# Retention, Mish layer and GELU layer in one kernel: two weight chunks in retention, second parts on GpSimd, scores of two units together

## The chip, the cores and the metric

The kernel runs on one core of a Trainium2 chip. The metric is the device time of one execution in microseconds (us), the median of three runs. The program is written out in full: every engine has its own list of instructions in a fixed order, and waits only where an instruction needs something that another engine or a transfer has not finished.

## The reference

Three steps, in float32. Retention: for each of 4 batches and 8 heads, scores of 576 positions, times a causal decay, times the values. Then two feed-forward layers over the 2304 tokens, the first with Mish, the second with a sigmoid form of GELU.

```python
scores = scale * np.matmul(q, k.transpose(0, 1, 3, 2))     # (4, 8, 576, 576), head size 64
Dmat = np.where(rel >= 0, gamma[:, None, None] ** rel, 0)  # gamma of each head
attn = np.matmul(scores * Dmat, v)
x = attn.transpose(0, 2, 1, 3).reshape(2304, 512)
h = x @ w_in;  x = (h * np.tanh(softplus(h))) @ w_out      # 512 -> 2048 -> 512
h = x @ w_in2; x = (h / (1 + np.exp(-1.702 * h))) @ w_out2 # 512 -> 2048 -> 512
```

## The kernel before, in words

**Retention** works in 20 units: 4 batches of 5 chunks of the sequence, four of 128 positions and a last one of 64 (units 4, 9, 14 and 19). One transfer brings a unit's q, k, v and k again (`load`, line 715). A unit goes through these steps: GpSimd multiplies v by its decay in place (`decay_v`, line 767); TensorE forms the scores (`scores`, line 778) and VectorE masks them into `pm` (line 782); TensorE adds the unit's keys and values to the running sum of its batch (`update`, line 801, not for the 64 wide chunk); ScalarE copies that sum to the state (`take`); TensorE forms the outputs from the state of the unit before (line 829, not for the first chunk of a batch) and from `pm` and v (line 840); VectorE scales them into X (`finish`, line 854). Five buffers hold units, so the load of unit u+4 waits for the last outputs of unit u-1. `pm` has four buffers, two per unit, and the scores use four banks, two per unit.

The scores of unit u+1 are issued ahead of the sum and the outputs of unit u, from unit 2 on.

**The Mish layer's inputs** are held as two parts, a rounded one and the rest: ScalarE writes the first part of X, VectorE subtracts it from X for the second (`split_x`, line 335). This is done for one quarter of the first token block in each of units 4 to 7 (512 columns), and for the second block in units 8 to 11 (256 columns).

**The Mish layer's weights** come in 16 chunks (`w1`, 1 MB each; tile `raw`). Each half of a chunk goes through six steps, tied by named places in the program ("vector", "act early", "pool", "act late"): VectorE clamps it (line 183), ScalarE does two conversions, VectorE does two integer steps (lines 128 and 195), GpSimd joins them (line 199), ScalarE writes the first part, VectorE subtracts for the second (line 236). In each pass of the unit loop, a place runs what is due there, so a half moves about one unit per step. The first three chunks are converted during retention: `fetch` at units 0, 4 and 8, the conversion's first step 5 units later. The other chunks are due at `LATE`, in steps of the Mish layer, where step 2m needs chunk m.

In one pass of the unit loop, GpSimd's list gets `decay_v(u + 1)`, then the joins that are due. VectorE's gets the masks of the unit whose scores are issued there, `finish(u)`, then the conversion steps, then the input's second part. ScalarE's gets `take(u)`, the conversions, the write of a first part of weights, then the input's first part.

**The Mish layer** starts at the end of retention: `up(0)` is issued after unit 17, `up(1)` after unit 18, then `layers()` alternates `up(i)` (line 348) and `down(i - 3)` (line 369). The GELU layer (lines 592 and 637) follows. Neither is touched by the change, other than by the due times of the weight chunks.

Of the kernel before, what the change touches and what calls it, by code (L numbers as in the profile page):

```python
# [22 lines left out]
NK = DM // P  # L23
NM = DFF // P
# [8 lines left out]
SIDE, WIDTH = 1, 256  # L33
# [26 lines left out]

KEPT = 10
X_UNITS = (4, 5, 6, 7, 8, 9, 10, 11)
EARLY = 3
EARLY_EVERY, EARLY_AFTER = 4, 5
LATE = [1 + 1.95 * i for i in range(NM - EARLY)]
UNITS_AHEAD = 4
GROW = (16, 32, 64)
TABLES = NCH * H + NPAIR * (NCH + len(GROW) + GROW[0])
# [29 lines left out]
def retention_mish_gelu_kernel(ctx: ExitStack, tc: tile.TileContext, qkv, w1, w2, tables, out):  # L98
    nc = tc.nc
# [57 lines left out]
    def place(m):  # L157
        return keep if m < KEPT else late[0]

    def fetch(m):  # L160

        raw = place(m + 1).tile([P, 2 * DM], I64, tag=f"w{m + 1}", name="raw")
        if m < EARLY:
            nc.sync.dma_start(out=raw, in_=w1[m])
# [128 lines left out]
    n_u = len(UNITS)  # L293
# [3 lines left out]
    def plan_conversion(m, s, every):  # L297

        for i in range(2):
            last[0] = max(math.ceil(s + i * every / 2), last[0] + (i == 0))  # L300
            plan("fetch" if m == NM - 1 else "vector", last[0] - (m == NM - 1), convert(m, i))

    for m in range(EARLY):
        u = EARLY_EVERY * m
        plan("fetch", u - n_u, fetch(m))
        plan_conversion(m, u + EARLY_AFTER - n_u, 2)
    for m, s in zip(range(EARLY, NM), LATE):
        if m < NM - 1:
# [15 lines left out]
    def split_x(t, k):  # L324

        o, n = BLOCKS[t]
        if t == SIDE:
            if k % 2 == 0:
                side.append(keep.tile([P, 2, 2, WIDTH], F32R, tag=f"side{k // 2}", name="side"))
            x = side[-1][:, k % 2]  # L330
        else:
            x = keep.tile([P, 2, NB], F32R, tag=f"x{k}", name=f"x{k}")
        xs[t, k] = x
        act(x[:, 0, :n], X[:, k, o : o + n])
        return lambda: nc.vector.tensor_tensor(  # L335
            out=x[:, 1, :n], in0=X[:, k, o : o + n], in1=x[:, 0, :n].bitcast(F32), op=ALU.subtract
        )

# [360 lines left out]
    def attention():  # L699
        with tc.tile_pool(name="att", bufs=1) as ap:  # L700
# [59 lines left out]
                load(u)  # L760
            pm, sums, now = {}, [None], [None]

            def decay_v(u):
                b, c = UNITS[u]
                n = CH[c][1]
                vv = loaded[u][2][:n].rearrange("p (h d) -> p h d", d=D)
                nc.gpsimd.tensor_tensor(
                    out=vv, in0=vv, in1=vt[:n, c, :].unsqueeze(2).to_broadcast([n, H, D]), op=ALU.mult
                )

            def scores(u):
                n = CH[UNITS[u][1]][1]
                qt, kt = loaded[u][:2]
                sc = [quarters(bank("sc", (0, 1, 2, 3))) for _ in range(2)]
                for p in range(NPAIR):
                    for j in range(2):
                        sl = slice(64 * j, 64 * j + 64)
                        nc.tensor.matmul(sc[j][:n, p, :n], lhsT=kt[sl, p, :], rhs=qt[sl, p, :], start=True, stop=True)  # L778
                pm[u] = []
                for j in range(2):  # L780
                    t = ap.tile([P, NPAIR, P], F32, tag="pm", name="pm", bufs=4)
                    nc.vector.tensor_tensor(  # L782
                        out=t[:n, :, :n],
                        in0=sc[j][:n, :, :n],
                        in1=cm[:n, :n].unsqueeze(1).to_broadcast([n, NPAIR, n]),
                        op=ALU.mult,
                    )
                    pm[u].append(t)
# [67 lines left out]
                )  # L856

            scores(0)
            decay_v(0)
            for u in range(n_u):  # L860
                step = u - n_u
                load(u + UNITS_AHEAD)
                if u + 1 < n_u:
                    decay_v(u + 1)
                position("pool", step)
                position("fetch", step)
                if 1 < u < n_u - 1:
                    scores(u + 1)
                update(u)
                now[0], before = take(u), now[0]  # L870
                o = outputs(u, before)
                if u == 1:
                    scores(u + 1)
                if u < NCH - 1:
                    n = CH[u + 1][1]
                    for p in range(NPAIR):
                        act(gt[:, u + 1, p, :n], gt[:, 0, p, :n], scale=steps[:, p, u + 1 : u + 2])
                position("act early", step)

                if u == n_u - 2:  # L880
                    elementwise(0, jobs=False)
                finish(u, o)
                if u == n_u - 1:
                    elementwise(1, jobs=False)
                if u == 0:
                    scores(1)
                position("vector", step)
                position("act late", step)
                if u in X_UNITS:
                    k = X_UNITS.index(u)  # L890
                    split_x((0, SIDE)[k // NK], k % NK)()
                if u == n_u - 3:
                    up(0)
                if u == n_u - 2:
                    up(1)
# [97 lines left out]
```

## Time and profile before

| | |
|---|---|
| median of 3 runs | 821.23 us (820.43 to 821.35) |
| the profiled execution | 821.12 us |
| its span | 819.4 us, 1.7 us below its time |
| TensorE busy in the span | 811.4 us, 99% |
| VectorE, ScalarE, GpSimd busy | 550.1, 406.2, 113.2 us |
| granted TensorE clock | the top digit, 9, in all of the page's 40 slices |
| chain that ended last | TensorE 93%, DMA 3%, VectorE 3% |

The span is the time in which the profile saw instructions. The chain that ended last is followed back from the last instruction to what released each step; it says which engine a moment of the span belongs to. Busy time of TensorE alone says little here, since matmuls are pipelined and a matmul that waits in the array counts as busy.

### The profile page before, as it was taken

How to read it: one execution, taken by the hardware profiler on the slowest of the kernel's cores; microseconds unless marked ns; L12 is line 12 of the kernel's file. 1: busy time of each engine (PE TensorE's matmuls, PEld its weight loads, DVE VectorE, ACT ScalarE, POOL GpSimd, SP SyncE). 2: the span in 40 equal slices, each digit the busy share in tenths (PEclk: the TensorE clock that was granted, in tenths of full speed). 3: DMA queues.
4: the chain of work that ended last, by engine and by line, in shares of the span. 5: the costliest groups of instructions: out<-in, count | busy, mean ns of one | idle time of the engine just before them, and what ended most of it. 6: DMA issues, size and time to landing. Idle time of an engine off the chain costs nothing.

```text
span 819.4 us, 13441 instructions
## 1 busy us (share of the span) xinstructions
PE 811.4 (99%) x5094; PEld 740.3 (90%) x5094; DVE 550.1 (67%) x1030; ACT 406.2 (50%) x748; POOL 113.2 (14%) x123
## 2 busy tenths in 40 slices
PE   8999999999999999999999999999999999999998
PEld 6888888888888888788888899999999999999998
DVE  4895566665876766787655455789645798555776
ACT  4553666664455556455443333465233665233553
POOL 3552222222122212133210000000000000000000
PEclk9999999999999999999999999999999999999999
DMA  9999700003477739678621277777877887877775
GB/s 344 400 334 368 281 1 2 1 1 103 142 239 221 246 116 257 193 202 264 188 78 64 102 261 251 258 259 252 325 250 237 274 272 256 306 252 247 261 266 168
DMA packets 96048, 175.01 MB, mean 214 GB/s; under 512 B 5232, under 2 KB 67312, under 8 KB 90096
## 3 DMA queue, kind: packets, MB, share of 16 engines
q1 hardware_dynamic: 95696, 173.89, 63.4%
q8 instruction: 40, 0.66, 0.3%
q10 hardware_dynamic: 288, 0.27, 0.1%
q14 instruction: 24, 0.20, 0.1%
HBM read 140.05 MB, written 34.08 MB: 213 GB/s over the span
## 4 chain that ended last, share of the span: by engine, by line
PE 93%; DMA 3%; DVE 3%; POOL 0%; issue 0%; ACT 0%; SPq 0%; POOLq 0%; DVEq 0%
PE h L348 24%; PE acc L369 23%; PE p L592 21%; PE p L637 21%; DMA unit<-qkv_dram 2%; PE o L840 1%; PE sc L778 1%; DVE pm L782 1%; PE o L829 1%; DMA stream<-cy 1%; PE ds L801 1%; DVE x L335 0%; DVE X L854 0%; DVE w L236 0%; DVE side L335 0%
## 5 line engine op out<-in xcount | busy, mean ns | idle before, releaser
L369 PE MATMUL acc<-g,w 128*128 128x512 f32 (+1 forms) x960 | 209.5, 368 | 0.0
L369 PEld LDWEIGHTS acc<-g,w 128*128 128x128 f32 x960 | 168.3, 188 | 30.4
L348 PE MATMUL h<-x,w 128*128 128x512 f32 x768 | 184.9, 390 | 0.3 <-DVE x L335 0.2
L592 PE MATMUL p<-xop,ring 128*128 128x384 f32 x1008 | 175.2, 334 | 0.0
L637 PE MATMUL p<-g,ring 128*128 128x384 f32 x1008 | 175.2, 334 | 0.0
L592 PEld LDWEIGHTS p<-xop,ring 128*128 128x128 f32 x1008 | 174.8, 188 | 0.1
L637 PEld LDWEIGHTS p<-g,ring 128*128 128x128 f32 x1008 | 174.8, 188 | 0.0
L348 PEld LDWEIGHTS h<-x,w 128*128 128x128 f32 x768 | 143.8, 188 | 31.0 <-DVE x L335 1.1
L398 DVE TENSOR_TENSOR g<-c,g 128x512 fp32r<-128x512 f32 x80 | 53.2, 664 | 110.2 <-ACT g L119 110.2
L119 ACT ACTIVATE g<-cs 128x384 fp32r<-128x384 f32 x168 | 87.9, 524 | 63.2 <-PE p L637 61.2
L430 DVE TENSOR_TENSOR g<-cs,g 128x384 fp32r<-128x384 f32 x168 | 92.5, 557 | 26.1 <-ACT g L119 25.0
L119 ACT ACTIVATE g<-c 128x512 fp32r<-128x512 f32 x80 | 47.1, 589 | 123.3 <-PE acc L369 122.9
L119 ACT ACTIVATE cs<-cs 128x384 f32<-128x384 f32 x72 | 37.9, 526 | 111.8 <-DVE cs L430 111.8
L199 POOL TENSOR_TENSOR cy<-cr 128x256 int32<-128x256 int32 x64 | 51.9, 831 | 177.5 <-DVE cr L195 96.5
L119 ACT ACTIVATE c<-h 128x512 f32<-128x512 f32 x80 | 44.1, 551 | 47.4 <-PE h L348 44.9
L430 DVE TENSOR_TENSOR cs<-cs 128x384 f32<-128x384 f32 x96 | 53.1, 553 | 0.8
L199 POOL TENSOR_TENSOR raw<-raw 128x512 int32<-128x512 int32 x30 | 34.4, 1147 | 98.5 <-DVE raw L195 93.1
L119 ACT ACTIVATE cr<-cr 128x512 int32<-128x512 uint32 x68 | 41.5, 664 | 1.3 <-DVE cr L183 1.3
L430 DVE TENSOR_TENSOR u<-p,s 128x384 f32<-128x384 f32 x30 | 16.7, 556 | 34.9 <-PE p L592 34.9
L119 ACT ACTIVATE raw<-raw 128x512 int32<-128x512 uint32 (+1 forms) x60 | 37.8, 674 | 4.6 <-DVE raw L183 4.4
L284 DVE TENSOR_TENSOR cy<-cy,cr 128x896 fp32r<-128x896 f32 x32 | 36.8, 1155 | 2.7 <-ACT cr L119 1.7
L277 DVE TENSOR_TENSOR cy<-cy 128x128 f32<-128x128 f32 x96 | 26.1, 299 | 13.3 <-POOL cy L199 12.2
(63 smaller groups left out, 644.6 us busy)
## 6 DMA issues: line engine op xcount, KB each, us to landing
ring<-stream SPq DMA_DIRECT2D x112, 512.0 KB, 4.5
ring<-stream SPq DMA_DIRECT2D x28, 1024.0 KB, 4.8
cr<-w_dram SPq DMA_DIRECT2D x34, 512.0 KB, 4.4
unit<-qkv_dram SPq DMA_DIRECT2D x15, 1024.0 KB, 8.2
stream<-cr SPq DMA_DIRECT2D x32, 448.0 KB, 2.8
stream<-cy SPq DMA_DIRECT2D x32, 448.0 KB, 3.3
raw<-w_dram SPq DMA_DIRECT2D x24, 512.0 KB, 10.4
raw<-w_dram SPq DMA_DIRECT2D x3, 1024.0 KB, 10.5
```

The source lines that it names most:

```text
L119: nc.scalar.activation(out=o, in_=i, func=f, scale=scale, bias=bias)
L199: nc.gpsimd.tensor_tensor(out=o, in0=upper, in1=bits, op=ALU.add)
L277: nc.vector.tensor_tensor(out=v[:, o], in0=v[:, a], in1=v[:, b], op=op)
L284: nc.vector.tensor_tensor(out=y, in0=v, in1=hi.bitcast(F32), op=ALU.subtract)
L348: nc.tensor.matmul(h[:, :n], lhsT=W[m][:, a, k * P : (k + 1) * P], rhs=xs[t, k][:, b, :n], start=((k, a, b) == order[0]), stop=((k, a, b) ...
L369: nc.tensor.matmul(acc[t, e][:, :n], lhsT=W[m][:, a, DM + e * P : DM + (e + 1) * P], rhs=g[:, b, :n],  start=(begins(i) and a == 0 and b = ...
L398: lambda: nc.vector.tensor_tensor(out=g[:, 1, :n], in0=c[:, :n], in1=g[:, 0, :n].bitcast(F32), op=ALU.subtract),
L430: eng.tensor_tensor(out=o, in0=a, in1=b, op=op)
L592: nc.tensor.matmul(banks[p], lhsT=w[:, a, k * P : (k + 1) * P], rhs=x[:, b, k], start=(p not in SAME and k == 0 and a == 0 and b == 0), st ...
L637: nc.tensor.matmul(banks[e, p], lhsT=w[:, a, e * P : (e + 1) * P], rhs=g[:, b], start=(p != 2 and r == 0 and a == 0 and b == 0), stop=(r = ...
L778: nc.tensor.matmul(sc[j][:n, p, :n], lhsT=kt[sl, p, :], rhs=qt[sl, p, :], start=True, stop=True)
L782: nc.vector.tensor_tensor(out=t[:n, :, :n], in0=sc[j][:n, :, :n], in1=cm[:n, :n].unsqueeze(1).to_broadcast([n, NPAIR, n]), op=ALU.mult,)
```

## The change

The table of early chunks is cut to two (the second fetched at unit 6, not 4), and the later chunks' due times start three steps earlier, so that chunk 2 is due at step -2, which is unit 18. The second parts of the inputs go to GpSimd. The decay of unit 0's v goes to VectorE. From unit 2 on, the scores are issued for two units together, behind the outputs of every even unit.

```diff
-EARLY = 3
-EARLY_EVERY, EARLY_AFTER = 4, 5
-LATE = [1 + 1.95 * i for i in range(NM - EARLY)]
+EARLY = 2
+EARLY_EVERY, EARLY_AFTER = 6, 5
+LATE = [-2 + 1.95 * i for i in range(NM - EARLY)]
...
-        return lambda: nc.vector.tensor_tensor(
+        return lambda eng=nc.vector: eng.tensor_tensor(
             out=x[:, 1, :n], in0=X[:, k, o : o + n], in1=x[:, 0, :n].bitcast(F32), op=ALU.subtract
         )
...
-            def decay_v(u):
+            def decay_v(u, eng=nc.gpsimd):
...
-                nc.gpsimd.tensor_tensor(
+                eng.tensor_tensor(
...
-            decay_v(0)
+            decay_v(0, nc.vector)
...
-                if 1 < u < n_u - 1:
-                    scores(u + 1)
                 update(u)
                 now[0], before = take(u), now[0]
                 o = outputs(u, before)
                 if u == 1:
                     scores(u + 1)
+                elif u and u % 2 == 0:
+                    for n in (u + 1, u + 2):
+                        if n < n_u:
+                            scores(n)
...
-                    split_x((0, SIDE)[k // NK], k % NK)()
+                    split_x((0, SIDE)[k // NK], k % NK)(nc.gpsimd)
```

GpSimd's list around units 8 to 10. The `unit` rows are the decays of units 8, 9 and 10, the `raw` rows the joins of the two halves of weight chunk 0. Before:

```order
L767 TENSOR_TENSOR unit_306<-unit_306,tab_75 128x512
L199 TENSOR_TENSOR raw_118<-raw_118 128x512
L767 TENSOR_TENSOR unit_346<-unit_346,tab_75 64x512
L199 TENSOR_TENSOR raw_118<-raw_118 128x512
L767 TENSOR_TENSOR unit_389<-unit_389,tab_75 128x512
```

and with the change (here the decays of units 8, 9 and 10 are `unit_306`, `unit_358` and `unit_387`; `x3` and `side` are second parts of the input):

```order
L767 TENSOR_TENSOR unit_306<-unit_306,tab_75 128x512
L199 TENSOR_TENSOR raw_118<-raw_118 128x512
L335 TENSOR_TENSOR x3_494<-X_60,x3_494 128x512
L767 TENSOR_TENSOR unit_358<-unit_358,tab_75 64x512
L199 TENSOR_TENSOR raw_118<-raw_118 128x512
L335 TENSOR_TENSOR side_559<-X_60,side_559 128x256
L767 TENSOR_TENSOR unit_387<-unit_387,tab_75 128x512
```

Each decay now stands behind a subtraction, which reads what ScalarE wrote.

VectorE's list from the masks of unit 7 to the first integer steps on chunk 0. Before (`sc_392` and `sc_393` are the scores of unit 7, `o_416` the outputs of unit 6):

```order
L335 TENSOR_TENSOR x1_386<-X_60,x1_386 128x512
L782 TENSOR_TENSOR pm_402<-sc_392,cm_76 128x512
L782 TENSOR_TENSOR pm_404<-sc_393,cm_76 128x512
L854 TENSOR_TENSOR X_60<-o_416,gt_79 128x4x128
L128 SCALAR_TENSOR_TENSOR raw_118<-raw_118 128x512
L195 TENSOR_SCALAR raw_118<-raw_118 128x512
L183 TENSOR_SCALAR raw_118<-raw_118 128x512
L335 TENSOR_TENSOR x2_439<-X_60,x2_439 128x512
```

and with the change (`sc_419`, `sc_420` are unit 7's scores, `sc_433`, `sc_434` unit 8's, `o_402` and `o_470` the outputs of units 6 and 7):

```order
L183 TENSOR_SCALAR raw_118<-raw_118 128x512
L782 TENSOR_TENSOR pm_429<-sc_419,cm_76 128x512
L782 TENSOR_TENSOR pm_431<-sc_420,cm_76 128x512
L782 TENSOR_TENSOR pm_443<-sc_433,cm_76 128x512
L782 TENSOR_TENSOR pm_445<-sc_434,cm_76 128x512
L854 TENSOR_TENSOR X_60<-o_402,gt_79 128x4x128
L128 SCALAR_TENSOR_TENSOR raw_118<-raw_118 128x512
L195 TENSOR_SCALAR raw_118<-raw_118 128x512
L183 TENSOR_SCALAR raw_118<-raw_118 128x512
L854 TENSOR_TENSOR X_60<-o_470,gt_79 128x4x128
```

The subtractions are gone, and the integer steps of chunk 0 stand behind the masks of two units.

TensorE's list from the scores of unit 6 on, over the sums and outputs of units 5 and 6. Before:

```order
L778 MATMUL sc<-unit 128x128 x8
L801 MATMUL ds<-unit 64x64 x8
L840 MATMUL o<-pm,unit 64x128 x8
L778 MATMUL sc<-unit 128x128 x8
L801 MATMUL ds<-unit 64x64 x8
L829 MATMUL o<-unit,state_72 64x128 x8
L840 MATMUL o<-pm,unit 64x128 x8
```

and with the change (the first row is the scores of units 5 and 6):

```order
L778 MATMUL sc<-unit 128x128 x16
L801 MATMUL ds<-unit 64x64 x8
L840 MATMUL o<-pm,unit 64x128 x8
L801 MATMUL ds<-unit 64x64 x8
L829 MATMUL o<-unit,state_72 64x128 x8
L840 MATMUL o<-pm,unit 64x128 x8
L778 MATMUL sc<-unit 128x128 x16
```

The scores of two units stand together, and those of unit 7 now come behind the outputs of unit 6.

## Rows read from the trace of the kernel before

**Rows 1.** Busy time by stretch: engine busy us (instructions), granted clock, DMA share, GB/s

```profile
22.00:37.00 15.00, 14.87 (x290) 13.49 (x290) 13.34 (x23) 8.42 (x17) 6.42 (x6) 1.00 1.02 393
37.00:58.00 21.00, 20.39 (x372) 17.80 (x370) 20.82 (x37) 10.68 (x22) 13.30 (x10) 1.00 0.97 368
...
420.00:620.00 200.00, 200.00 (x1093) 192.01 (x1092) 122.52 (x216) 83.02 (x156) 0.00 (x0) 1.00 0.64 218
```

**Rows 2.** The chain of waits, TensorE and DMA pieces: start us, length us, what

```profile
9.93 11.97 DMA unit<-qkv_dram
...
24.51 1.16 PE sc L778 x16
...
30.62 1.09 PE sc L778 x16
31.71 0.61 PE ds L801 x16
32.33 0.88 PE o L829 x16
33.20 0.87 PE o L840 x16
34.08 0.61 PE sc L778 x16
...
66.17 2.97 PE h L348 x12
...
72.12 1.63 PE h L348 x12
73.74 0.62 PE o L829 x16
...
74.97 4.38 PE h L348 x24
79.35 2.75 PE acc L369 x12
```

**Rows 3.** The same chain, VectorE pieces between 43 and 54 us

```profile
43.82 1.20 DVE pm L782 x2
45.02 0.60 DVE X L854
45.62 0.61 DVE raw L128
...
46.25 0.43 DVE raw L195
46.68 0.34 DVE raw L183
...
53.81 0.74 DVE pm L782 x2
```

**Rows 4.** GpSimd's instructions on tiles unit and raw: ns min/median/max

```profile
L767 POOL TENSOR_TENSOR unit<-unit,tab x20: 1035/1043/1897, 7.1 to 64.8; 128x512 f32<-128x512 f32 x16, 64x512 f32<-64x512 f32 x4
...
L199 POOL TENSOR_TENSOR raw<-raw x6: 1041/1150/1414, 32.5 to 62.8; 128x512 int32<-128x512 int32 x6
```

**Rows 5.** Timeline of ScalarE, 30 to 40 us: start us, length us, instruction

```profile
30.88 0.61 ACT L119 ACTIVATE x<-X 128x512 fp32r<-128x512 f32 x1
...
38.59 0.70 ACT L119 ACTIVATE w<-raw 128x512 fp32r<-128x512 f32 x1 [2.18 <-POOL raw L199]
39.18 0.73 ACT L119 ACTIVATE side<-X 128x256 fp32r<-128x256 f32 x2
```

**Rows 6.** Timeline of VectorE, unit 0's masks and two subtractions of one form

```profile
7.42 1.29 DVE L782 TENSOR_TENSOR pm<-sc,cm 128x512 f32<-128x512 f32 x2 [0.61 <-PE sc L778]
...
24.88 1.25 DVE L335 TENSOR_TENSOR x<-X,x 128x512 fp32r<-128x512 f32 x1
...
28.30 0.68 DVE L335 TENSOR_TENSOR x<-X,x 128x512 fp32r<-128x512 f32 x1
```

**Rows 7.** The first matmuls of the program, line 745: ns min/median/max

```profile
L745 PE MATMUL unused<-state x6: 593/1061/1222, 1.5 to 5.6; 128*128 128x512 f32 x6
```

## The prediction

> **What bounds the kernel now.** I read busy time by stretch first, then the chain of waits, then the timelines of the engines that hand work to each other. From the end of retention on there is nothing to win: TensorE is busy in every microsecond of 420 to 620 [rows 1], and the chain that ended last is TensorE's alone. So only retention, the first 75 us, can change, and with it the first steps of the Mish layer, where weights are still being converted. In 22 to 37 us TensorE is busy 14.87 of 15 us; in 37 to 58 VectorE is busy 20.82 of 21 and TensorE slips [rows 1].
>
> How much TensorE slips, I get from the chain [rows 2]. One unit costs it 1.09 (scores) + 0.61 (sum) + 0.88 + 0.87 (outputs) = 3.45 us; the first unit of a batch lacks the 0.88, and a 64 wide unit has 0.61 + 0.62 + 0.62 and no sum. Between the scores of unit 6 at 24.51 and `up(0)` at 66.17 stand 11 wide scores, 2 narrow ones, 11 sums and the outputs of units 5 to 17: 13.2 + 6.7 + 19.1 = 39.0 us. The stretch took 41.66, so **2.7 us** are lost there, nearly all while VectorE is full. From 66.17 to 74.97 nothing is lost: `up(0)`, `up(1)`, the rest of units 18 and 19 add up to 8.8. Before 24.51 data set the time: the chain shows 11.97 us of one load from 9.93 on [rows 2], and the DMA engines are still at a share of 1.02 in the next stretch [rows 1]. So I take 24.5 as the moment at which unit 6 can be had.
>
> **The change, part by part.**
>
> *First batch, unit 0's decay: 0.* On VectorE the decay stands behind two masks: these start at 7.42 [rows 6] and take 1.2 [rows 3], the product 0.6 more (0.68 for a like form [rows 6], of which 0.08 lies beside the next one). So unit 0's sum starts at 9.2. From there to the scores of unit 6 TensorE has 0.61 + 0.87 for unit 0, 3 x 3.45, 0.61 + 1.24 for unit 4 and 1.09 for the scores of unit 5, 14.8 us, which end at 24.0, and unit 6 comes at 24.5. If that cover of 0.5 us fails, the cost is at most the same 0.5. The second score of a pair waits for its own load: for unit 6 it is this same 24.5, later ones have slack, since a unit takes TensorE 3.45 us, and 1.05 MB at the 393 GB/s of this stretch [rows 1] is 2.7 us.
>
> *Fetches: 0.* Chunk 2 goes behind the last load and chunk 1 two loads later on SP's queue. Both only bring units earlier; what TensorE waited for units behind 24.5 is within the 2.7 us below.
>
> *VectorE relieved: -2.7.* It loses chunk 2's conversion and eight subtractions. I let all 2.7 us go. Pairs by themselves cost nothing: the mask of a pair's first unit has 1.09 + 0.61 + 0.88 = 2.6 us until TensorE wants it and takes 1.3. In units 4 to 7 GpSimd has a decay and a subtraction per unit, some 2.1 of 3.45 us, and nothing to wait for but ScalarE's copy: nothing either. What is late next stands in the following items.
>
> *GpSimd at units 8 to 10: +4.6.* This is the term that decides. GpSimd's list now reads join, x3's second part, decay 9, join, side's second part, decay 10. A second part waits for ScalarE's first part, which stands on ScalarE behind the write of the weight that waits for the join before. So GpSimd waits for ScalarE, which waits for GpSimd, and the decays, which TensorE needs, stand at the end. A walk with the row durations, from 24.51:
>
> TensorE: scores of unit 6 until 25.7, the rest of units 5 and 6 until 29.5, scores of 7 and 8 until 31.7, units 7 and 8 until 36.4, scores of 9 and 10 until 38.1, first outputs of 9 until 38.7. Then it needs decay 9, and 0.6 later decay 10.
>
> VectorE: masks of 7 and 8 from 30.7, 2.4; X of unit 6, 0.6; only then chunk 0's integer steps, 1.06 [rows 3]: done at 34.8. In the program of before these stood ahead of unit 8's masks.
>
> GpSimd and ScalarE: join 1.04 [rows 4] to 35.8; weight 0.70 [rows 5] to 36.5; x3 0.61 to 37.1; GpSimd's subtraction to 38.2; decay 9 1.04 to 39.2; second join to 40.2; weight 0.70 to 40.9; side 0.37 to 41.3; subtraction 0.52 to 41.8; decay 10 to 42.9.
>
> So TensorE waits 0.5 for decay 9, and, being ready at 39.8, 3.1 for decay 10: 3.6 us. The price of a subtraction on GpSimd is in no row. Its nearest ones are the decay, 1043 ns of float32 at the same size, and the join, 1041 at best [rows 4]; I take 1.04, and half of it for 256 columns. Ends: VectorE's own 0.68 [rows 6] takes 0.5 off the walk. Upwards, a GpSimd instruction can be held by VectorE: the decay's longest is 1897 [rows 4], 0.85 over its median, and a VectorE subtraction beside GpSimd took 1.25 against 0.68 [rows 6]. One such wait and the hand-overs give 4.6; two give 5.4. If VectorE gets to the integer steps sooner, 2.0 remain. Range 2.0 to 5.4.
>
> *Units 15 and 16: +1.5.* Chunk 1 is now converted in units 11 to 16. From the end of unit 13's scores until TensorE wants unit 15's mask it has 0.61 + 2.36 + 1.24 + 1.09 + 1.09 + 0.61 = 7.0 us. VectorE has masks of 13, 14 and 15 (1.20, 0.74, 1.20), X of 12 and 13 (1.20), two pairs of integer steps (2.12) and a clamp (0.34) [rows 3]: 6.80. That is a margin of 0.2 which one hold of 0.57 or 0.85 breaks, and ScalarE's copy of unit 15's state stands behind a weight that waits for a join. 0 to 2.0; I take two holds.
>
> *First steps of the Mish layer: +1.2.* Chunk 2 must be ready when `up(4)` is issued. Counted from the end of unit 18's outputs, TensorE has 0.61 + 1.63 + 1.24 + 4.38 + 2.75 = 10.6 us [rows 2]. Chunk 2's first half starts behind X of unit 18 (unit 19's scores 0.61 and masks 0.74, the second part of `up(0)`'s result and X 0.6 each: 2.6 after), goes through clamp, ScalarE, integer steps behind X of unit 19 (5.8), join (6.9), weight (7.6), then behind Mish, first part and second part of `up(2)`'s result (its end is at 6.2 to 6.5, then about three times 0.6 with ScalarE's turn; 9.6) to the subtraction at 10.2. With a hold or two it ends at 11 to 11.5. Chunk 3 follows in the same steps with both halves together. So 0 to 0.8 each; I take 0.6 twice.
>
> *Sum:* -2.7 + 4.6 + 1.5 + 1.2 = +4.6 us. The profiled execution took 821.12 (span 819.4 and 1.7 around it), 0.1 below the median of 821.23. **825.7 us.** The low ends give 820.4, the high ends 827.4.
>
> **Weighed against the Trainium skill.** In the trace TensorE's granted clock is 1.00, the 2.4 GHz level, in both stretches of retention that I show, but TensorE was busy for 14.87 of 15 and 20.39 of 21 us in them [rows 1]. Its very first matmuls, after idle, took 1061 ns in the median and 593 at the shortest for one form [rows 7]. The Trainium skill, in "TensorE: Matmul & The Clock Gate", section "Part 1: The HAM clock gate (the "warmup" mystery)", says that an idle TensorE is put back to 1.2 GHz and must earn the full clock again. By the rows alone the sum stays 825.7; by that rule it is the third rival's.
>
> **Rivals.**
>
> 1. *GpSimd is in time* (8 in 100). GpSimd is busy only 13.30 of 21 us in 37 to 58 [rows 1], so there is room for 6.4 us more. Then only the relief counts: 821.1 - 2.7 = 818.4, faster. It decides by one point: decay 10 must end at 39.8, 3.1 us before my walk. Against it: the walk's wait is made of order, not of load.
> 2. *The two cancel* (10 in 100). GpSimd's wait is near its lower end and the two smaller terms are nothing or nearly so: 821.1 - 2.7 + 2.0 + up to 1.5, about 821.5, no difference that a measurement of this kernel tells (0.2%, 1.6 us).
> 3. *The clock falls in the wait* (15 in 100). The 3 us in front of unit 10 put TensorE to 1.2 GHz. A unit of 3.45 us at 1061/593 of its time [rows 7] costs 2.7 more: 828.4. Against it: the waits are short and 0.6 us of work lies between them.
>
> That the change does not do what it says can only hold for the fetches, which I count at nothing.
>
> **How the numbers follow.** My forecast, with its bounds, has 67 in 100 and lies at 823 to 827.5. With the third rival, slower by over 0.2% (above 822.8) has 82 in 100, no difference 10, faster (below 819.5) 8. The range leaves out the first rival, part of the second and the far end of the third: 821.9 to 829.2.
>
> **What would show it.** Right: TensorE's unit 10 sum (line 801) waits some 3 us for GpSimd's decay (line 767), with GpSimd waiting for ScalarE in line 335 ahead of it; masks (line 782) or the state copy late near units 15 and 16; small waits of `up(4)` and `up(6)` for line 236; the stretch up to `up(2)` ends near 78, not 74.97. Wrong: decay 10 ending by 40, VectorE still above 95% busy between 37 and 58, or a granted clock below 1.00 after unit 10.

## The result and the profile after

| | before | after |
|---|---|---|
| median | 821.28 us (820.43 to 821.35, 4 runs) | 829.64 us (829.43 to 829.74, 4 runs) |
| the profiled execution, its span | 821.12, 819.4 us | 829.71, 827.9 us |
| mean granted TensorE clock | 1.000 | 0.994 |

The change is slower: ratio 1.0105, 95% interval 1.0092 to 1.0118, which is 8.4 us. I had predicted 825.7 with a range up to 829.2. The direction was right, and the time lies 0.4 us above the range.

I followed the loss along TensorE's timeline by three marks. The scores of unit 6 began at 24.51 and now begin at 26.50: 2.0 us. From there to `up(0)` it took 41.60 (24.51 to 66.11) and now takes 47.60 (26.50 to 74.10): 6.0 us. From `up(0)` to `up(2)` nothing is lost, 8.8 us in both. From `up(2)` to the sixth `down` it took 26.43 and now takes 27.08: 0.65 us. Behind that the two run alike to 0.2 us.

TensorE's timeline of after, with the waits behind each row (start us, length us, instruction, in brackets the idle time before it and what ended it; the first row is the matmuls with which the program starts, whose result nothing reads):

```profile
1.52 5.49 PE L745 MATMUL unused<-state 128*128 128x512 f32 x6 [1.52 <-DVE state L724]
...
10.16 0.95 PE L801 MATMUL ds<-unit 128*64 128x64 f32 x16 [2.05 <-DVE unit L767]
10.88 1.93 PE L840 MATMUL o<-pm,unit 128*64 128x128 f32 x16
...
29.21 0.88 PE L840 MATMUL o<-pm,unit 128*64 128x128 f32 x12 [0.74 <-issue]
...
32.23 2.06 PE L778 MATMUL sc<-unit 64*128 64x128 f32 x32
34.21 0.69 PE L801 MATMUL ds<-unit 128*64 128x64 f32 x16
...
42.43 0.68 PE L840 MATMUL o<-pm,unit 64*64 64x64 f32 x16 [0.86 <-POOL unit L767]
46.49 1.12 PE L801 MATMUL ds<-unit 128*64 128x64 f32 x16 [3.38 <-POOL unit L767]
47.41 1.92 PE L840 MATMUL o<-pm,unit 128*64 128x128 f32 x16
49.26 3.05 PE L778 MATMUL sc<-unit 64*128 64x128 f32 x32
52.23 0.69 PE L801 MATMUL ds<-unit 128*64 128x64 f32 x16
52.75 1.05 PE L829 MATMUL o<-unit,state 128*64 128x128 f32 x16
53.62 1.04 PE L840 MATMUL o<-pm,unit 128*64 128x128 f32 x16
...
64.36 0.69 PE L801 MATMUL ds<-unit 128*64 128x64 f32 x16 [0.35 <-POOL unit L767]
65.24 0.43 PE L840 MATMUL o<-pm,unit 128*64 128x128 f32 x2 [0.20 <-DVE pm L782]
65.84 1.09 PE L840 MATMUL o<-pm,unit 128*64 128x128 f32 x14 [0.17 <-DVE pm L782]
67.39 0.69 PE L801 MATMUL ds<-unit 128*64 128x64 f32 x16 [0.46 <-ACT state L119]
```

The two large waits are where the prediction put them: 0.86 us for unit 9's decay and 3.38 us for unit 10's. But the rows around them show something that the sum did not hold. Unit 0's outputs take 1.93 us instead of 1.04, unit 10's sum 1.12 instead of 0.69, and a pair's scores 3.05 instead of 2.06. Busy time by stretch shows why (columns as in [rows 1]; the granted clock stands behind the five engines). The first row is before, the others are after:

```profile
5.00:22.00 17.00, 15.13 (x259) 12.86 (x257) 9.38 (x18) 7.94 (x24) 5.21 (x5) 1.00 1.01 404
...
5.00:22.00 17.00, 14.95 (x211) 12.12 (x209) 7.35 (x14) 6.11 (x18) 4.54 (x4) 0.90 1.01 403
...
37.00:58.00 21.00, 16.68 (x278) 15.17 (x276) 12.16 (x21) 8.33 (x18) 12.72 (x13) 0.84 0.67 248
44.00:46.00 2.00, 0.00 (x0) 0.00 (x0) 0.86 (x2) 0.68 (x3) 1.55 (x2) 0.64 0.77 284
46.00:48.00 2.00, 1.50 (x22) 1.51 (x24) 0.00 (x0) 0.27 (x1) 2.00 (x3) 0.50 0.21 77
48.00:50.00 2.00, 2.00 (x20) 1.67 (x18) 0.00 (x0) 0.90 (x3) 1.10 (x3) 0.50 0.02 4
50.00:52.00 2.00, 2.00 (x28) 2.00 (x26) 0.63 (x2) 0.00 (x0) 0.75 (x1) 0.66 0.76 217
52.00:54.00 2.00, 2.00 (x46) 1.88 (x44) 2.00 (x5) 0.99 (x3) 0.00 (x0) 1.00 0.73 307
```

TensorE idles from 43.11 to 46.49; inside that wait the granted clock falls to 0.50, the 1.2 GHz level, and it stays there for most of the next 5 us of work. From unit 10's sum to the next unit's sum TensorE needed 52.23 - 46.49 = 5.74 us. At the full clock the same instructions take 0.52 + 0.87 + 1.98 = 3.4 (52.23 to 52.75 for a sum, 52.75 to 53.62 for one set of outputs, 32.23 to 34.21 for the scores of a pair): 2.4 us lost. The clock of 0.90 between 5 and 22 us is a second fall, behind the wait of 2.05 us in front of unit 0's sum. In before, the clock is 1.00 both there and between 37 and 58 [rows 1]. VectorE fell from 20.82 to 12.16 us busy between 37 and 58: it no longer sets the pace there, the wait for GpSimd does.

Why GpSimd was late, in its own timeline of after:

```profile
37.65 1.15 POOL L199 TENSOR_TENSOR raw<-raw 128x512 int32<-128x512 int32 x1 [2.14 <-DVE raw L195]
40.11 1.27 POOL L335 TENSOR_TENSOR x<-X,x 128x512 fp32r<-128x512 f32 x1 [1.32 <-ACT x L119]
41.34 1.03 POOL L767 TENSOR_TENSOR unit<-unit,tab 64x512 f32<-64x512 f32 x1
42.34 1.03 POOL L199 TENSOR_TENSOR raw<-raw 128x512 int32<-128x512 int32 x1
44.45 0.99 POOL L335 TENSOR_TENSOR side<-X,side 128x256 fp32r<-128x256 f32 x1 [1.08 <-ACT side L119]
45.41 1.04 POOL L767 TENSOR_TENSOR unit<-unit,tab 128x512 f32<-128x512 f32 x1
```

and ScalarE's beside it:

```profile
38.83 0.69 ACT L119 ACTIVATE w<-raw 128x512 fp32r<-128x512 f32 x1 [0.17 <-POOL raw L199]
39.41 0.62 ACT L119 ACTIVATE x<-X 128x512 fp32r<-128x512 f32 x1
...
43.41 0.67 ACT L119 ACTIVATE w<-raw 128x512 fp32r<-128x512 f32 x1 [2.57 <-POOL raw L199]
43.98 0.70 ACT L119 ACTIVATE side<-X 128x256 fp32r<-128x256 f32 x2
```

GpSimd waits for ScalarE's first part (lines 335 and 119), which stands behind a weight that waits for GpSimd's join; the decay that TensorE needs is last, and unit 10's starts only at 45.41. This is the prediction's walk, with each step ending 2.9 to 3.6 us later (the first join at 38.8 for 35.8, unit 10's decay at 46.4 for 42.9), of which 2.0 are the first batch.

And VectorE's, where the list of two masks holds the integer steps back:

```profile
33.42 2.48 DVE L782 TENSOR_TENSOR pm<-sc,cm 128x512 f32<-128x512 f32 x4 [2.06 <-PE sc L778]
...
36.42 0.68 DVE L128 SCALAR_TENSOR_TENSOR raw<-raw 128x512 int32<-128x512 int32 x1
37.14 0.43 DVE L195 TENSOR_SCALAR raw<-raw 128x512 int32<-128x512 int32 x1
```

VectorE was idle for 2.06 us in front of these masks. The integer steps that the first join needs stood behind them in its list.

### The profile page after: what moved, and what is told of

Its sections match the earlier page's. It is cut to its first block, busy times and chain, and to the rows that moved or that the text cites. A ratio compares the mean times of both kernels' runs of the same rounds, so it can differ in the third digit from the quotient of the medians.

```text
span 827.9 us, 13461 instructions
## 1 busy us (share of the span) xinstructions
PE 814.3 (98%) x5094; PEld 743.2 (90%) x5094; DVE 550.1 (66%) x1023; ACT 405.7 (49%) x748; POOL 119.6 (14%) x130
## 4 chain that ended last, share of the span: by engine, by line
PE 91%; DVE 3%; issue 2%; POOL 2%; DMA 1%; ACT 1%; POOLq 0%; DVEq 0%; SPq 0%; ACTq 0%
PE h L348 22%; PE acc L369 22%; PE p L592 21%; PE p L637 21%; PE sc L778 1%; PE o L840 1%; POOL unit L767 1%; PE o L829 1%; DMA stream<-cy 1%; PE ds L801 1%; PE unused L745 1%; POOL raw L199 1%; DVE g L398 0%; DVE raw L128 0%; DVE x L335 0%
## 5 line engine op out<-in xcount | busy, mean ns | idle before, releaser
L398 DVE TENSOR_TENSOR g<-c,g 128x512 fp32r<-128x512 f32 x80 | 55.5, 694 | 102.8 <-ACT g L119 102.7
L782 DVE TENSOR_TENSOR pm<-sc,cm 128x512 f32<-128x512 f32 (+1 forms) x40 | 22.9, 629 | 24.5 <-PE sc L778 24.4
## 6 DMA issues: line engine op xcount, KB each, us to landing
raw<-w_dram SPq DMA_DIRECT2D x26, 512.0 KB, 10.1
```

Of the source, the lines that this page charges most:

```text
L398: lambda: nc.vector.tensor_tensor(out=g[:, 1, :n], in0=c[:, :n], in1=g[:, 0, :n].bitcast(F32), op=ALU.subtract),
L782: nc.vector.tensor_tensor(out=t[:n, :, :n], in0=sc[j][:n, :, :n], in1=cm[:n, :n].unsqueeze(1).to_broadcast([n, NPAIR, n]), op=ALU.mult,)
```

## The experiments

**Theory:** four places cost. (a) The order of GpSimd's list makes the decays of units 9 and 10 late; (b) the wait drops the clock; (c) unit 0's decay on VectorE opens a wait that drops the clock too; (d) the pairs push the joins back. **Rivals:** the pairs or the load on GpSimd cost by themselves; or the new due times of the weights do.

### Unit 0's decay back on GpSimd

```diff
-            decay_v(0, nc.vector)
+            decay_v(0)
```

> The changed kernel with unit 0's decay back on GpSimd. Order theory (the second parts in GpSimd's list hold up the decays of units 9 and 10, and the low clock behind unit 10 follows from that wait): the wait in front of unit 10's sum stays at 3 to 3.5 us, the half clock behind it stays, and only what the first batch lost may come back: the scores of units 5 and 6 end near 25.6 and not 27.5, 827.7 us. Rival (unit 0's decay is what opens the gap in which the clock falls, and the rest follows from the late start): the waits further on shrink as well, 825 us or less. Second rival (the first batch is late only because TensorE's first matmuls happened to run longer at the low clock, 5.49 against 4.71 us): no change, 829.6 us.

826.71 us (825.68 to 827.35, 4 runs), 1.0069 of before (1.0054 to 1.0084): 2.9 us less than the whole change, and 1 us less than the theory had. Its first batch loses nothing (scores of unit 6 at 24.33, clock 1.00 between 5 and 22), and the wait in front of unit 10 and the slow instructions behind it are unchanged:

```profile
43.79 1.12 PE L801 MATMUL ds<-unit 128*64 128x64 f32 x16 [3.38 <-POOL unit L767]
```

So the loss in the first batch is one thing and the loss at unit 10 another. The second rival is out too: the first scores start at 6.84 here, nearly as late as in after (6.94; before 6.16), and the batch still ends in time.

### Each decay one unit earlier in GpSimd's list

```diff
-                if u + 1 < n_u:
-                    decay_v(u + 1)
+                for n in (1, 2) if u == 0 else (u + 2,):
+                    if n < n_u:
+                        decay_v(n)
```

> The changed kernel with every decay put one unit earlier into GpSimd's list, ahead of the second part it stood behind. Same work on every engine. Order theory: the waits of 0.9 and 3.4 us in front of units 9 and 10 fall to 0 to 1.3 us, the clock stays at 2.4 GHz there, and 829.6 becomes 822 to 823.5 us (4.2 less for the waits, 2.4 less for the clock). Rival (GpSimd has too much to do in units 7 to 12, and holds against VectorE make it longer): the wait moves to units 11 to 13 and stays at 3 us or more, 828 us or more.

822.22 us (820.28 to 824.26, 10 runs), 1.0016 of before (1.0004 to 1.0027): 7.4 us less than the whole change. Order alone gives 6.4 of it: from unit 6's scores to `up(0)` it takes 41.24 us (27.44 to 68.68) against 47.60 in after and 41.60 in before. The rest comes from the first batch, which seems to have kept the full clock in four of the ten runs (820.28 to 821.33 at a mean clock of 1.000; the others 822.01 to 824.26 at 0.997 or 0.998). GpSimd does the same work as in the change. Its timeline now has unit 9's decay ahead of the first join and unit 10's ahead of the second, while the join, the subtraction and its wait for ScalarE stand as they were:

```profile
34.85 1.03 POOL L767 TENSOR_TENSOR unit<-unit,tab 64x512 f32<-64x512 f32 x1
37.93 1.15 POOL L199 TENSOR_TENSOR raw<-raw 128x512 int32<-128x512 int32 x1 [2.04 <-DVE raw L195]
40.42 1.27 POOL L335 TENSOR_TENSOR x<-X,x 128x512 fp32r<-128x512 f32 x1 [1.35 <-ACT x L119]
41.66 1.04 POOL L767 TENSOR_TENSOR unit<-unit,tab 128x512 f32<-128x512 f32 x1
42.66 1.04 POOL L199 TENSOR_TENSOR raw<-raw 128x512 int32<-128x512 int32 x1
```

Unit 10's sum waits 0.26 us instead of 3.38, and the clock between 37 and 58 us is 1.00. Theory (a) holds: the loss at units 9 and 10 was order, not load.

### Second parts back on VectorE

```diff
-                    split_x((0, SIDE)[k // NK], k % NK)(nc.gpsimd)
+                    split_x((0, SIDE)[k // NK], k % NK)()
```

> The changed kernel with the inputs' second parts back on VectorE. Order theory: GpSimd's list has no instruction that waits for ScalarE, the waits for decays in units 9 and 10 fall below 1 us and the clock stays up; VectorE has 8 subtractions more, so TensorE waits up to 2 us in all for masks in units 9 to 12; 823 to 825 us. Rival (scores in pairs are what makes TensorE wait, since a mask has half the time): waits for masks of 4 us or more, 827 us or more.

826.12 us (824.70 to 826.44, 4 runs), 1.006 (1.0043 to 1.0077): 3.5 us less than the change, and 1 us more than I had expected. The decay of unit 10 is 0.57 us late instead of 3.38 and the clock behind it stays at 1.00, but TensorE now waits in front of unit 9's outputs (0.71 us, which the trace puts down to no engine; they start at 41.63, 0.5 us after VectorE began unit 9's masks at 41.12) and for unit 11's mask on VectorE (0.67). That pointed to the pairs, tested below. In the first batch of this execution the clock fell as in after (0.90 between 5 and 22).

### Filler work in front of unit 10

```diff
+                if u == 9:
+                    filler = ps.tile([P, NB], F32, tag="b5", name="filler")
+                    for _ in range(4):
+                        nc.tensor.matmul(filler, lhsT=cm, rhs=gt[:, 0], start=True, stop=True)
```

> The changed kernel with four float32 matmuls of 128x512 into a free bank, which nothing reads, between unit 9's outputs and unit 10's sum: TensorE works through most of the wait. Clock theory (the half clock behind unit 10 is the price of the idle time before it, 2.4 us): the wait for decay 10 shrinks to about a microsecond, unit 10's sum starts when it did (46.5 us), the granted clock is 1.00 from 44 to 52, and 829.6 becomes 827.2 us. Rival (the clock falls for another reason, or units 10 to 12 are slow because of what VectorE still has to do): 829.6 us or more.

825.17 us (824.18 to 826.58, 4 runs), 1.0053 (1.0038 to 1.0068). More work, and less time than the change by 4.5 us, 2 us more than I had expected from the clock behind unit 10 alone. TensorE's timeline of the profiled run (824.18 us; each filler matmul is recorded as two):

```profile
39.88 0.68 PE L840 MATMUL o<-pm,unit 64*64 64x64 f32 x16 [0.83 <-POOL unit L767]
40.49 3.70 PE L894 MATMUL filler<-gt,cm 128*128 128x512 f32 x8
44.13 0.69 PE L801 MATMUL ds<-unit 128*64 128x64 f32 x16
...
47.60 0.69 PE L801 MATMUL ds<-unit 128*64 128x64 f32 x16
```

The sum of unit 10 starts no sooner than without the filler (4.25 us behind the start of unit 9's outputs against 4.06 in after), and the decay is as late as it was: it ends 4.02 us behind that start in both. What went is the slow stretch: 44.13 to 47.60, where the next sum starts, are 3.47 us against after's 5.74. That shows (b) by itself, 2.3 us. In the first batch this execution kept the full clock (scores of unit 6 at 24.43, not 26.50), which is another 2.1. Two of the four runs did so by their mean clock (824.18 and 824.31 us at 1.000 and 0.999, 826.03 and 826.58 at 0.998), so the 4.5 us of the median mix both.

### Scores of one unit at a time

```diff
+                if 1 < u < n_u - 1:
+                    scores(u + 1)
...
-                elif u and u % 2 == 0:
-                    for n in (u + 1, u + 2):
-                        if n < n_u:
-                            scores(n)
```

> The change with its pairs undone: scores of one unit at a time again. Theory (the order of GpSimd's list makes the wait, the pairs only add to it): chunk 0's integer steps on VectorE come ahead of unit 8's masks again, so the first join and with it decay 10 end some 1 us earlier; TensorE still waits 2 to 3 us in front of unit 10 and unit 0's decay still opens its gap of 2 us: 826.5 to 828.5 against 829.6. Rival (the pairs are what makes GpSimd late): no wait over 1 us in front of unit 10, no fall of the clock there, 825 or less.

824.16 us (821.34 to 826.10, 6 runs), 1.0042 (1.0026 to 1.0057): 5.5 us less than the change, 2 us more than the theory had. By its time alone the rival holds, but the wait of over 2 us and the fall of the clock are still there, which the rival had not. Part of the 5.5 is the first batch again: the three runs whose mean clock is as low as the change's (0.993 or 0.994) took 825.06 to 826.10, and from unit 6's scores to `up(0)` the profiled run took 43.52 us (24.36 to 67.88) against 47.60. So undoing the pairs is worth 4.1. TensorE's timeline (the profiled run, 823.27 us):

```profile
43.38 1.12 PE L801 MATMUL ds<-unit 128*64 128x64 f32 x16 [2.06 <-POOL unit L767]
44.29 1.92 PE L840 MATMUL o<-pm,unit 128*64 128x128 f32 x16
46.14 1.21 PE L778 MATMUL sc<-unit 64*128 64x128 f32 x16
```

The waits in front of units 9 and 10 are 0.57 + 2.06, 1.6 us less than in after. The slow clock ends sooner: unit 10's sum and outputs are slow (43.38 to 46.14, 2.8 us where 1.4 would do), the next scores are not, so the clock takes 1.4 us and not 2.4. The 1.2 us of waits at units 15 and 16 are gone. VectorE now has the integer steps ahead of unit 8's masks:

```profile
32.21 1.40 DVE L195 TENSOR_SCALAR raw<-raw 128x512 int32<-128x512 int32 x1
...
34.71 1.28 DVE L782 TENSOR_TENSOR pm<-sc,cm 128x512 f32<-128x512 f32 x2
```

So the first join starts at 34.47, 10.1 us behind the scores of unit 6; in after it was 37.65, 11.15 us behind them: the pairs push it back by 1 us. In this execution the first sum waits 2.05 us as in after, yet the scores of unit 6 start at 24.36: the wait alone is hidden.

### Two weight chunks alone, on the kernel before

```diff
-EARLY = 3
-EARLY_EVERY, EARLY_AFTER = 4, 5
-LATE = [1 + 1.95 * i for i in range(NM - EARLY)]
+EARLY = 2
+EARLY_EVERY, EARLY_AFTER = 6, 5
+LATE = [-2 + 1.95 * i for i in range(NM - EARLY)]
```

> The kernel before with two early weight chunks and the new due times, and nothing else of the change. Theory (the relief of VectorE is real and is worth about 2 us up to the second step of the Mish layer, and about 1 us is given back where chunks 2 and 3 are due): 819.5 to 820.5, about 1 us faster than before; granted clock 1.00 throughout retention; no wait over 1 us in front of units 9 and 10. Rival (the new due times are themselves too late or collide): small waits of units 15 and 16 and of the fifth and seventh steps of the Mish layer add up to more than the relief, 822 or more.

819.62 us (819.40 to 820.33, 11 runs), 0.999 of before (0.9981 to 0.9999): 1.0 us faster, the only version here whose interval lies below 1. From unit 6's scores to `up(0)` it takes 40.16 us (24.49 to 64.65) against 41.60: the relief of VectorE by one chunk is worth 1.4 us, and 0.4 us of it go where chunks 2 and 3 are due. VectorE is less full, 19.86 us busy instead of 20.82:

```profile
37.00:58.00 21.00, 20.62 (x390) 18.25 (x390) 19.86 (x37) 9.75 (x21) 12.65 (x11) 1.00 0.93 339
```

### Three list edits together: decays ahead, unit 0's decay on GpSimd, scores one at a time

The edits of three runs above, made together on the change:

```diff
-            decay_v(0, nc.vector)
+            decay_v(0)
...
-                if u + 1 < n_u:
-                    decay_v(u + 1)
+                for n in (1, 2) if u == 0 else (u + 2,):
+                    if n < n_u:
+                        decay_v(n)
...
+                if 1 < u < n_u - 1:
+                    scores(u + 1)
...
-                elif u and u % 2 == 0:
-                    for n in (u + 1, u + 2):
-                        if n < n_u:
-                            scores(n)
```

> The change with three edits: each decay one unit earlier in GpSimd's list, unit 0's decay back on GpSimd, scores of one unit at a time. Theory (these three are all that the change loses by): no wait over 0.6 us in front of units 9 and 10, clock 1.00 from the first batch on, the relief of VectorE of two conversions left over: 819 to 820.5, faster than before by about 1 us. Rival (GpSimd's subtractions hold VectorE through the port they share, or units 15 and 16 and the Mish layer's first steps take it back): 821.5 to 823.

820.61 us (820.38 to 821.00, 11 runs), 0.9999 (0.9991 to 1.0008). The whole loss is gone, and nothing is gained over before, against the 1 us that the theory had: the second parts on GpSimd bring nothing here.

### Pairs and two chunks

```diff
-            decay_v(0, nc.vector)
+            decay_v(0)
...
-                    split_x((0, SIDE)[k // NK], k % NK)(nc.gpsimd)
+                    split_x((0, SIDE)[k // NK], k % NK)()
```

> The change with the second parts on VectorE and unit 0's decay on GpSimd, so that pairs and two chunks are left. Theory (the costs of unit 0's decay and of the second parts on GpSimd add up, each worked out from its own run: 3.5 us and 2.9 us of the 8.4): 823.0 to 823.7 (829.6 - 3.5 - 2.9), clock 1.00 from the first batch on. Rival (they share one loss, the clock): 825 or more; second rival (pairs and two chunks cost nothing by themselves): 821 or less.

824.06 us (823.42 to 825.81, 5 runs), 1.0045 (1.0033 to 1.0057): 0.9 us above the sum of the two single effects (823.2), 0.4 above the stated range, and far from the rival by which pairs cost nothing. Beside two chunks alone the pairs cost 4.4 us (4.1 between the marks: 24.58 to 68.86 is 44.28 us, against 40.16). VectorE has a pair's masks behind its other work and TensorE waits for them. A row of TensorE's timeline:

```profile
47.17 0.43 PE L840 MATMUL o<-pm,unit 128*64 128x128 f32 x2 [0.61 <-DVE pm L782]
```

and VectorE's timeline ahead of it, where the masks begin only when the second parts of a weight and of the input are through:

```profile
44.72 1.46 DVE L236 TENSOR_TENSOR w<-raw,w 128x512 fp32r<-128x512 f32 x1
...
46.44 2.47 DVE L782 TENSOR_TENSOR pm<-sc,cm 128x512 f32<-128x512 f32 x4
```

### Pairs and two chunks, with the decays ahead

On the kernel of the last experiment:

```diff
-                if u + 1 < n_u:
-                    decay_v(u + 1)
+                for n in (1, 2) if u == 0 else (u + 2,):
+                    if n < n_u:
+                        decay_v(n)
```

> Pairs and two chunks, second parts on VectorE, unit 0's decay on GpSimd, and each decay one unit earlier in GpSimd's list. Pairs cost 4.4 us there without the last edit. Theory (most of it is VectorE's: a pair's masks stand behind its backlog, and the first of them has less lead; the waits for GpSimd's decays in front of units 10 and 15 were 0.56 and 0.37): 822.5 to 823.5. Rival (it is GpSimd's: the masks hold back the integer steps, those the joins, those the decays): 821 or less.

823.28 us (822.47 to 824.38, 5 runs), 1.0032 (1.0019 to 1.0045). Only 0.8 us better, so little of the pairs' cost is GpSimd's. Most of what is left points to VectorE: waits of 0.59, 0.33 and 0.61 us end on it, and unit 9's outputs, whose wait of 0.73 the trace puts down to no engine, start 0.5 us after VectorE began unit 9's masks (41.22, 40.71). In the profiled run (824.15 us) the clock also fell, in the first batch: a pair's second scores, unit 6's, waited 1.82 us for their load, then took 1.91 us instead of 1.16, and the clock is 0.89 between 22 and 37. The pairs open that wait (1.29 and 1.17 us in the runs before and after this one, at full clock).

### The whole change but unit 0's decay, with the decays ahead

On the change:

```diff
-            decay_v(0, nc.vector)
+            decay_v(0)
...
-                if u + 1 < n_u:
-                    decay_v(u + 1)
+                for n in (1, 2) if u == 0 else (u + 2,):
+                    if n < n_u:
+                        decay_v(n)
```

> The change with each decay one unit earlier in GpSimd's list and unit 0's decay back on GpSimd; pairs, second parts on GpSimd and two chunks stay. Theory (pairs cost only where VectorE or GpSimd is behind; with VectorE relieved and the decays in time they cost nothing): the first batch ends at 24.4 us, and from there to the first step of the Mish layer it takes the 41.2 us that the run with the decays ahead showed: 820 to 821.3, no half clock. Rival (pairs cost some 4 us wherever they stand, as they did beside two chunks alone): 823.5 or more.

820.87 us (820.29 to 822.74, 11 runs), 1.0005 (0.9996 to 1.0014), against 820.61 with single scores. Where VectorE is relieved and the decays are in time, the pairs cost nothing that these runs tell. Together with the two experiments before: the pairs take away lead, and cost where VectorE or GpSimd is behind.

### Unit 0's decay on VectorE alone, on the kernel before

```diff
-            decay_v(0)
+            decay_v(0, nc.vector)
```

> The kernel before with unit 0's decay on VectorE and nothing else. Theory (the decay opens a gap of 2 us in front of the first sum; the wait itself hides behind the first batch's transfers, and only a fall of the clock behind it costs): the gap is there in every run; where the clock stays full, the scores of unit 6 still start at 24.4 to 24.6 and the time is that of before; where it falls, they start near 26.5 and the time is 822.5 to 823.5. So single runs between 820.5 and 823.5, in two groups. Rival (the wait itself costs, whatever the clock does): all runs at 822 or more. Second rival (the clock falls only because of something else in the change): all runs within 0.5 us of before.

821.98 us (820.39 to 823.40, 11 runs), 1.0014 (1.0005 to 1.0023), in two groups by the clock, as expected. Five runs with a mean clock of 0.999 or 1.000 took 820.39, 820.60, 820.97, 821.06 and 821.55; six with 0.997 or 0.998 took 821.98 to 823.40. The profiled run is of the first group. It has the wait, and still hardly a loss at the end of the batch (scores of unit 6 at 24.85, where before has 24.51) and a clock of 1.00:

```profile
9.34 0.69 PE L801 MATMUL ds<-unit 128*64 128x64 f32 x16 [2.05 <-DVE unit L767]
```

So the wait itself is hidden but for 0.3 us, and the fall of the clock behind it is not. Whether it falls differs from run to run of one kernel; in the four runs of the change, at 829.43 to 829.74 and a mean clock of 0.993 to 0.994, it seems to have fallen each time.

The kept traces show one thing that goes with it. Of the six profiled runs with unit 0's decay on VectorE, the clock fell at that wait in the three in which TensorE's first matmuls ended late, so that the first scores start at 6.93 or 6.94 (after, decays ahead, second parts on VectorE). It held in the three in which they start at 6.12 to 6.47 (this run, single scores, filler). Six runs are few, and none was made to test this, so the cause stays open.

### Two chunks alone, with the decays ahead

On the kernel with two chunks alone:

```diff
-                if u + 1 < n_u:
-                    decay_v(u + 1)
+                for n in (1, 2) if u == 0 else (u + 2,):
+                    if n < n_u:
+                        decay_v(n)
```

> The kernel before with two early chunks and the new due times, and each decay one unit earlier in GpSimd's list. Theory (two chunks alone left only 0.36 us of waits behind 24.5 us, so there is nearly nothing for earlier decays to win): 819.3 to 819.9, no difference from two chunks alone. Rival (GpSimd's decays still set hidden waits): 819 or less.

820.33 us (820.00 to 820.92, 11 runs), 0.9995 (0.9986 to 1.0004): a miss in both directions, since its median is 0.7 us above that of two chunks alone, though the two intervals against before overlap. The traces show a place. From unit 6's scores to `up(0)` it takes 40.91 us against 40.16. Unit 9's decay now runs on GpSimd from 31.11 to 32.15, beside VectorE's integer step on chunk 0, and that step takes 1.44 us:

```profile
31.26 1.44 DVE L128 SCALAR_TENSOR_TENSOR raw<-raw 128x512 int32<-128x512 int32 x1
```

With two chunks alone GpSimd has nothing at that time and the step takes 0.69. What follows on VectorE is 0.8 us later (unit 10's masks at 41.36 for 40.60), and TensorE waits 0.60 us for a mask instead of 0.20. So an earlier decay is not free where nothing waited for it.

## Why the prediction was right and wrong

**GpSimd at units 8 to 10, +4.6: right.** The waits are 0.86 + 3.38 = 4.2 us, at the two places and with the chain that the walk gave. In it the price of a subtraction was short: 1.27 us, and 0.73 at best for 256 columns, where I took 1.04 and half of it. The hold that I added did not come at a decay or a join (1.03 to 1.15 us each); its 1.0 us happened to cover the subtractions' price and the hand-overs. The run with the decays ahead shows that order makes the wait. But this term stops when TensorE starts again, and there the next one begins.

**The clock falls in the wait: left out of the sum, held as a rival at 15 in 100, and it is what happened.** This is the first step that failed. Its price was near (2.7 by [rows 7] against 2.4 measured), its chance was wrong; a granted clock below 1.00 after unit 10 was one of my signs of being wrong. My argument against it, that the waits are short with 0.6 us of work between, is refuted by the rows of after: idle for 0.86 and 3.38 us of some 4.9, TensorE lost the clock inside the second wait. The rule that I had named from the Trainium skill ("TensorE: Matmul & The Clock Gate", section "Part 1: The HAM clock gate (the "warmup" mystery)"), that an idle TensorE goes back to 1.2 GHz, is what the trace then showed.

**First batch, unit 0's decay, 0: wrong, by 2.0 us.** This is the second step that failed: I let a fall of the clock follow only the wait at unit 10 and not this one. The wait and its cover were about right. In the kernel of before with that edit the decay ends at 9.28, where I had 9.2, and at full clock the batch ends at 24.4 to 24.9. In after the decay ends later, at 10.10, since the first matmuls took 5.49 us (4.71 in before) and the first scores start 0.8 us later. The fall's own share is 1.6 us: from unit 0's sum to the scores of the pair 5 and 6 after takes 15.34 us (10.16 to 25.50), and the filler run, the same program up to there at full clock, 13.74 (9.68 to 23.42). The other 0.4 is the later sum, beyond the cover. In the medians, taking unit 0's decay back gave 2.9.

**"Pairs by themselves cost nothing": wrong as a general step.** I checked only that a mask takes less than TensorE's time until it is wanted. In the change the pairs push the first join back by 1 us, because VectorE sits idle in front of a pair's masks with the integer steps behind them; they lengthen the wait that drops the clock, and bring the waits at units 15 and 16. My walk held the first of these, which is why the term above came out, but the text called the pairs free. Undoing them alone gave back 4.1 us between the marks (5.5 in the medians), and beside two chunks alone they cost 4.4.

**VectorE relieved, -2.7: right in the sum, less in what can be had.** After's stretch from unit 6's scores to `up(0)` is 47.60; without the waits shown (0.74 + 0.86 + 3.38 + 0.35 + 0.20 + 0.17 + 0.46 = 6.2) and the 2.4 of the clock, 39.0 are left, the figure that the prediction had as TensorE's own time. But two chunks alone gave 1.4 us there, and the subtractions nothing more: with the decays ahead and single scores in both, 820.61 us with them on GpSimd stand against 820.33 with them on VectorE. The Trainium skill, "Perfetto Trace Analysis", section "Optimizing Scalar/DVE Operations", warns that GpSimd and VectorE share a read port, so that moving work between them may not help; these two times agree, though they do not show that the port is the reason.

**Units 15 and 16, +1.5, and the Mish layer's first steps, +1.2:** measured 0.35 + 0.20 + 0.17 + 0.46 = 1.2, and 0.65. Of the first, 0.83 are at the places that I named, the mask and the state copy; the 0.35 is a wait for a decay that I had not named. And the waits are the pairs': with single scores they are gone. The second was taken at twice its size.

**By the terms:** 2.0 (first batch) + 4.2 + 2.4 + 0.7 (the wait at 28.47 that the trace puts down to nothing) + 1.2 - 2.6 (relief, taken as what is left over between the marks) + 0.65 = 8.6, against 8.5 between the spans. My sum of +4.6 lacked the two falls of the clock, 2.4 + 1.6 = 4.0 us, which is nearly all of the 3.9 between 825.7 and 829.64; the smaller errors (first batch 0.4 and the wait at 28.47 on one side, units 8 to 10, 15 and 16 and the Mish layer on the other) cancel, and that is luck.

## What to carry to other kernels

Where an engine's list mixes short work that the bound engine waits for with work that waits for a third engine, put the first kind ahead by one round: here that alone took back the 6 us that retention had lost behind the first batch, with no work removed. Do it where something waits: on two chunks alone the same edit seems to have cost 0.7 us. When a change opens a wait of 2 to 3 us on TensorE, count the wait and what the clock may take behind it, and do so also where data would hide the wait itself. And issuing work in pairs cost nothing here only where the engine that serves the pair had slack; look in its list for what now stands behind both.

## What the runs showed of the hardware that was not expected

A wait of 2.05 us in front of the first sum was enough to drop its clock in some runs of one kernel and not in others: between two groups of the same kernel lie 0.4 to 3.0 us (821.98 to 823.40 against 820.39 to 821.55). In after the fall at unit 10 came inside a wait of 3.38 us, not behind it: the clock is 0.64 in the mean of 44 to 46. The Trainium skill ("TensorE: Matmul & The Clock Gate", section "Part 1: The HAM clock gate (the "warmup" mystery)") says that the chip's look at the activity does not start with the kernel, so that one kernel shows different cold stretches from run to run. The two groups agree with it, and so do the first matmuls, which are the same in every version and ended at different times (first scores at 5.77 to 6.94).

Filler matmuls whose result nothing reads took the slow stretch away. Of their own 3.70 us at most 0.2 went beyond the wait.

A subtraction of 128x512 whose result is rounded took GpSimd 1.27 us, and the decay of the same size 1.04 [rows 4].

An integer step of VectorE (128x512, line 128) took 1.44 us with a GpSimd decay beside it and 0.69 without.
